# Layer normalisation moved to GpSimd, a wider prologue, a reordered tail and a deeper weight prefetch in a two-layer transformer kernel

## The chip, the cores and the metric

The kernel runs on one core of a Trainium2 chip. The core has five engines that work side by side, each with its own queue: TensorE (PE in the profile; PEld is its weight load) multiplies matrices into PSUM, VectorE (DVE) and ScalarE (ACT) do elementwise work and read PSUM, GpSimd (POOL) does elementwise work in SBUF, and SyncE (SP) issues the DMA transfers, in order. Engines wait for each other through semaphores. The metric is the device time of one execution in microseconds (us), as the median of several runs.

## The reference

The program is two layers, each of an attention block and a feed-forward block, over x of 2048 rows and 512 columns (bf16), with 32 heads of 16 columns and 1792 hidden columns. The layers share their weights:

```python
h = layernorm(x)                       # no scale or shift
q, k, v = split(h @ wqkv)              # 32 heads of 16
x = x + concat(softmax(q @ k.T / 4) @ v) @ wo
x = x + silu(layernorm(x) @ w1) @ w2
```

Most of the elementwise work is the exponential of the scores: 2048 x 2048 for each of 32 heads and two layers, 268 million values.

## The kernel before

**Blocks and steps.** Scores are made transposed, in blocks of 128 keys by 512 queries, four heads at a time: four matmuls of 32 rows side by side on TensorE. A *step* of the main loop handles one key tile for four heads. Three of its four blocks go through ScalarE's exp (one 512-wide, bank `s1`, and one 1024-wide, two banks of `s2`; `exp`, L1182). The fourth, the *d block*, goes through VectorE (`emit_d`, L1091, bank `sd`): it writes the power of two as integer bits into a tile `d_y`, and GpSimd makes two more terms of each pair of d blocks (`other_terms`, L1112, tiles `d_z`); P@V on TensorE (`o_ps`, L960) adds the three terms with scaled copies `VB` of V. A list made in `plan` (L880 on) says which blocks belong to which step. `D_LEAD` = 4: d blocks are made four steps ahead of the others, and those of the first four steps are exps, in step 0. `NO_D` = 12: the blocks of steps 5 to 12 have no d block; all four go through ScalarE there, the second 512-wide one in the bank `sd`, while VectorE starts in that bank on the blocks that come later.

**Background work.** Everything else (projections of K, Q and V, layer norms, output projections, feed-forward) is cut into parts and placed between the steps. `Background` holds the parts in three lists (`outs`, the main queue, `side`), and in each step the loop near its end asks `heads` for candidates and places those that `fits` accepts. `Model` carries the planner's times of each engine for this; its order is written into the queues when the program is built, and the engines then follow it. `bg.ensure` places what a step can't do without.

**Layer norm.** `ln_stats` makes mean and variance on VectorE (L419, L421) and `rstd` on GpSimd with two small instructions (L423, L424). `ln_apply` (L430) normalises one 128x512 tile on VectorE; it works on 513 columns, for which each x tile has one more column, set to zero (L340). The result `xn` has three buffers and goes through a DMA transpose on SP's queue (`transpose`, L329) into `xnT` or `fT`.

**Prologue.** Before the main loop, x of the first 512 rows is loaded in two halves, and the weights in the order K, Q, V; then x of the next chunk. TensorE runs 56 small warm-up matmuls. The four tiles are normalised on VectorE, transposed on TensorE into two PSUM banks of two tiles each (`t_ps`, L1159), copied by ScalarE three times and by VectorE once (L1160), and K and Q of the first head group follow as whole 512-wide projections (`proj_k`, `proj_q`). `proj_q` masks Q twice on VectorE straight from PSUM (L524), for each head group of the first chunk.

**Feed-forward weights.** w1 comes in 14 tiles of 128 columns with three buffers. `next_w1` (L690 on) issues the load of tile ft+2 when the matmuls of tile ft are placed; two tiles are there when a feed-forward begins. In layer 1, from the third unit on, w1 stays in SBUF (`w1_here`).

**Tail.** After the last step `tail` (L785 on) does the last 256 rows alone: transposes of the attention output, the output projection (`out_add`, L638: projection in PSUM, VectorE adds x), statistics of both tiles together, normalise, transposes, then per hidden tile h, tanh on ScalarE (L665), product on VectorE (L668) and the second matmul three tiles behind, and the output. Warm-up matmuls fill gaps of TensorE.

The softmax here doesn't subtract the row's maximum and nothing guards it: scores larger than these inputs give would overflow.

## Time and profile before

| | us |
|---|---|
| median of three runs (1551.96 to 1555.56) | 1552.83 |
| the profiled execution | 1553.61 |
| its span, first to last instruction | 1551.8 |
| ScalarE busy / TensorE / GpSimd / VectorE | 1510.2 / 1456.6 / 1143.1 / 1036.6 |
| first exp starts | 16.07 |
| last P@V starts | 1523.21 |
| ScalarE, 1024-wide exps: 1013 in the normal steps, mean | 1.329 |
| ScalarE, 512-wide exps: 1013, mean | 0.902 |
| VectorE, d_y: 1012, mean | 0.690 |
| GpSimd, d_z 128x1024: 1012, about | 1.045 |
| VectorE, normalise: 64, shortest / median / longest | 0.374 / 0.484 / 1.251 |

Instructions of one engine overlap in the profile, so that the sum of durations is more than the busy time; what one instruction costs its engine is read from the distance between starts. A line of the order of time gives the start, the duration, the engine, the line of the kernel, the operation, the tiles written and read, and in brackets how long the engine was idle before it and what ended that.

### The profile page before, as it was taken

Reading aid. Unit: us, or ns where it says so; the run is one execution under the profiler, and the core shown is the slowest. Engines: PE = TensorE matmul, PEld = TensorE weight load, DVE = VectorE, ACT = ScalarE, POOL = GpSimd, SP = SyncE. Lnnn points to the kernel's source line nnn. Section 1 sums busy time; section 2 is a strip of 40 time slices with the busy share of each in tenths; the row PEclk is TensorE's granted clock in tenths of the full one; section 3 lists DMA queues with packets and bytes.
Section 4 is the critical chain, followed back from the end, with each engine's and each line's share of the span. In section 5 each row is a group of like instructions: output and inputs, shape, how many; then the busy total and the mean of one; then the engine's idle time right before and its main releaser. Section 6 shows DMA issues by size and latency. Waiting matters only on the chain. (4 is left out here: it accounts for less than half of the span.)

```text
span 1551.8 us, 39817 instructions
## 1 busy us (share of the span) xinstructions
PE 1456.6 (94%) x15947; PEld 535.6 (35%) x16056; DVE 1036.6 (67%) x1714; ACT 1510.2 (97%) x2185; POOL 1143.1 (74%) x1245
## 2 busy tenths in 40 slices
PE   8999999899989999899999999998999899999997
PEld 3222332232222332223332233322344344444544
DVE  5877667657676766666676667676567656665663
ACT  6999999999999999999999999999999999999994
POOL 2888777678876888678876678776778677777771
PEclk9999999999999999999999999999999999999999
DMA  4110012102121111211112010121023212000100
GB/s 136 36 28 2 5 36 61 43 15 45 39 49 32 33 24 39 52 28 41 19 40 45 22 35 5 28 49 42 18 47 89 54 25 40 21 21 16 22 14 10
DMA packets 144489, 54.42 MB, mean 35 GB/s; under 512 B 123312, under 2 KB 143792, under 8 KB 144304
## 3 DMA queue, kind: packets, MB, share of 16 engines
q1 hardware_dynamic: 144304, 51.88, 15.0%
q8 instruction: 125, 2.05, 0.6%
q14 instruction: 60, 0.49, 0.1%
HBM read 26.21 MB, written 4.19 MB: 20 GB/s over the span
## 5 line engine op out<-in xcount | busy, mean ns | idle before, releaser
L1182 ACT ACTIVATE p_sb<-s_ps 128x512 bf16<-128x512 f32 x2026 | 1469.2, 1115 | 2.1 <-PE d_ps L924 1.7
L1091 DVE TENSOR_SCALAR d_y<-d_ps 128x512 uint16<-128x512 f32 x1012 | 698.1, 690 | 440.3 <-PE d_ps L924 385.0
L924 PE MATMUL s_ps<-QT,KT 32*128 32x512 bf16 (+1 forms) x3852 | 642.7, 337 | 53.1 <-ACT p_sb L1182 39.1
L924 PEld LDWEIGHTS <-KT 32*128 32x128 bf16 x5120 | 202.2, 91 | 608.8 <-issue 567.5
L924 PE MATMUL d_ps<-QT,KT 32*128 32x512 bf16 (+1 forms) x1268 | 389.9, 339 | 3.4 <-DVE d_y L1091 2.8
L960 PE MATMUL o_ps<-p_sb,VA 128*32 128x512 bf16 (+1 forms) x3807 | 312.1, 343 | 7.1 <-ACT p_sb L1182 1.1
L960 PEld LDWEIGHTS <-VA 128*32 128x32 bf16 x5120 | 120.2, 95 | 136.8 <-issue 104.6
L960 PE MATMUL o_ps<-d_y,VA 128*32 128x512 f16 (+1 forms) x1268 | 154.2, 337 | 0.0
L960 PEld LDWEIGHTS <-VB 128*32 128x32 f16 x2536 | 98.2, 97 | 41.9 <-issue 0.5
L749 PE MATMUL f_ps<-w_sb,hT 128*128 128x512 bf16 x370 | 102.6, 382 | 5.5 <-issue 4.8
L665 ACT ACTIVATE t_sb<-h_ps 128x512 f32<-128x512 f32 x105 | 93.4, 889 | 3.6 <-PE h_ps L486 3.1
L668 DVE SCALAR_TENSOR_TENSOR hT<-t_sb,h_ps 128x512 bf16<-128x512 f32 x105 | 72.0, 685 | 22.2 <-ACT t_sb L665 20.6
L960 PE MATMUL o_ps<-w_qkv,zero 128*32 128x512 bf16 (+1 forms) x1356 | 73.3, 335 | 0.0
L1071 DVE CAST oT<-o_ps 128x512 bf16<-128x512 f32 (+1 forms) x80 | 46.0, 574 | 7.7 <-PE o_ps L960 7.7
L749 PEld LDWEIGHTS <-hT 128*128 128x128 bf16 x420 | 31.3, 97 | 47.9 <-issue 25.4
L419 DVE BATCH_NORM_STATS2 st<-x 128x6 f32<-128x512 bf16 x64 | 43.6, 681 | 1.9 <-DMA x<-in_A_x_dram 1.9
L430 DVE TENSOR_SCALAR xn<-x,mv,rstd 128x513 bf16<-128x513 bf16 x64 | 42.0, 670 | 1.9 <-POOL rstd L424 1.7
L960 PEld LDWEIGHTS <-zero 128*32 128x32 bf16 x1356 | 28.1, 95 | 27.1 <-issue 20.0
L486 PE MATMUL k_ps<-xnT,w_qkv 128*128 128x512 bf16 x128 | 36.0, 393 | 1.3 <-DMA xnT<-xn 0.7
L486 PE MATMUL q_ps<-xnT,w_qkv 128*128 128x512 bf16 x136 | 36.7, 388 | 0.0
L627 POOL TENSOR_TENSOR attn<-ot,rec 128x128 bf16<-128x128 bf16 (+1 forms) x61 | 31.2, 511 | 6.0 <-DVE rec L620 6.0
L486 PE MATMUL v_ps<-w_qkv,xnT 128*128 128x512 bf16 x112 | 33.0, 382 | 1.6 <-issue 0.6
(2279 smaller groups left out, 2074.9 us busy)
## 6 DMA issues: line engine op xcount, KB each, us to landing
QT<-q SPq DMA_DIRECT2D x240, 16.0 KB, 1.8
x<-in_A_x_dram SPq DMA_DIRECT2D x7, 512.0 KB, 4.3
wo<-in_A_wo_dram SPq DMA_DIRECT2D x6, 512.0 KB, 3.8
out_dram<-x SPq DMA_DIRECT2D x16, 128.0 KB, 1.7
w_sb<-in_B_w_dram SPq DMA_DIRECT2D x1, 1792.0 KB, 13.2
w_qkv<-in_A_wqkv_dram SPq DMA_DIRECT2D x3, 512.0 KB, 6.8
w_here<-in_B_w_dram SPq DMA_DIRECT2D x3, 512.0 KB, 5.1
ot<-oT SPq DMA_TRANSPOSE x61, 2.4
```

What stands on the lines that cost most here:

```text
L419: nc.vector.bn_stats(st[:], x_sb[c][:, i, :])
L430: nc.vector.tensor_scalar(out=wide[:].rearrange("p (a b) -> p a b", b=19), in0=x_wide[c][:, D * i : D * (i + 1) + 1], scalar1=mv[:, 0:1], ...
L486: nc.tensor.matmul(ps.rearrange("p (t q) -> p t q", q=P) if len(r.shape) == 3 else ps, lhsT=lhs(ct), rhs=r, start=(ct == 0), stop=(ct == C ...
L627: scale(out=attn[L, qc][:, 0:n, P * g : P * (g + 1)].rearrange("p t (j s) -> p t j s", s=32)[:, :, :, 16 * par : 16 * par + 16], in0=att[: ...
L665: nc.scalar.activation(t_sb, h_ps, ACT.Tanh, scale=0.5)
L668: nc.vector.scalar_tensor_tensor(out=out, in0=t_sb, scalar=1.0, in1=h_ps, op0=ALU.add, op1=ALU.mult)
L749: nc.tensor.matmul(y_ps, lhsT=hT[:, ft, k * P : (k + 1) * P], rhs=w2_sb[:, ft, :], start=(ft == 0), stop=(ft == FT - 1),)
L924: nc.tensor.matmul(out[:, P * len(q) * n : P * len(q) * (n + 1)], lhsT=KT[L, kts // 4][r, g, (kts % 4) * P : (kts % 4 + 1) * P], rhs=QT[g] ...
L960: nc.tensor.matmul(o_tiles[key][32 * j : 32 * j + 32, 0:w], lhsT=lhsT[k] if real else zero[:], rhs=rhs[:, w * k : w * (k + 1)], start=(n[j ...
L1071: nc.vector.tensor_copy(out=o, in_=o_tiles[key][:, 0 : o.shape[-1]])
L1091: nc.vector.tensor_scalar(out=pr["y"][:, len(pr["ds"]), :], in0=s_ps[:], scalar1=float(1024 * SCALE * math.log2(math.e)), scalar2=float(10 ...
L1182: nc.scalar.activation(p_sb, s_ps, ACT.Exp, bias=-SHIFT * math.log(2.0) + math.log(EXP_SUM), scale=float(SCALE),)
```

## The change

The normalise of the main loop runs on GpSimd (`ln_apply` takes an engine); the prologue and the tail keep VectorE. It works on 512 columns, the extra column of x is gone, and `xn` has four buffers. Of the second to fourth head group's Q, VectorE makes one copy and GpSimd the two masked ones (`q_masked`). The blocks of steps 5 to 8 keep four exps; for steps 9 to 12 the four d blocks become two 1024-wide exps placed ahead of step 9 (`lead`, `p_lead`), so the bank `sd` is VectorE's from step 9 on. In the prologue each of the four transposed tiles has its own bank, K and Q are made in halves of two tiles each, eight warm-ups stand between, and x of the second chunk is loaded ahead of V's weights. In the main loop the `side` list goes ahead of the main queue until the second chunk is normalised. w1's tiles are loaded three ahead, each load placed after the product of its unit. In the tail x is added in PSUM by a fifth matmul with the identity, statistics are read from PSUM tile by tile, each with its own `rstd`, and ScalarE copies the sum into x.

```diff
-    def heads(self, now):
-        return [
-            self.outs[0] if self.outs else None,
-            self.head(now),
-            self.prime(self.side[0]) if self.side else None,
-        ]
+    def heads(self, now, side_first=False):
+        heads = [self.head(now), self.prime(self.side[0]) if self.side else None]
+        return [self.outs[0] if self.outs else None, *heads[:: -1 if side_first else 1]]
...
-    xnpool = ctx.enter_context(tc.tile_pool(name="xnpool", bufs=3))
+    xnpool = ctx.enter_context(tc.tile_pool(name="xnpool", bufs=4))
...
-    def transpose(out, in_):
+    def transpose(out, in_, made=0.0):
         nc.sync.dma_start_transpose(out=out, in_=in_)
         if bg.model:
+            bg.model.sp = max(bg.model.sp, made)
             bg.model.transpose()
...
-        x_wide[c] = xpool.tile([P, 4 * D + 1], BF16, name="x", tag="x")
-        nc.gpsimd.memset(x_wide[c][:, 4 * D :], 0.0)
-        x_sb[c] = x_wide[c][:, 0 : 4 * D].rearrange("p (t d) -> p t d", t=4)
...
         nc.sync.dma_start(w_qkv[:, :, D * i : D * (i + 1)], wq[:, :, D * i : D * (i + 1)])
-    load_x(1)
+        if i == 0:
+            load_x(1)
...
+    def ln_apply(c, i, mv, rstd, engine=nc.vector):
+        xn = xnpool.tile([P, D], BF16, name="xn", tag="xn")[:]
+        engine.tensor_scalar(
+            out=xn,
+            in0=x_sb[c][:, i, :],
             scalar1=mv[:, 0:1],
             scalar2=rstd,
             op0=ALU.subtract,
...
     def ln_chunk(c, dst, tiles=range(4)):
         for i in tiles[::2]:
             mv, rstd = stats.pop((c, i))
-            yield part(need=("rstd", c, i))
             for u in range(2):
-                yield part(0.45, need=("xn", xn_count[0] - XN_BUFS))
-                xn = ln_apply(c, i + u, mv[:, u, :], rstd[:, u, :])
-                transpose(dst[:, i + u, :, :], xn)
+                yield part(need=("xn", xn_count[0] - XN_BUFS))
+                xn = ln_apply(c, i + u, mv[:, u, :], rstd[:, u, :], nc.gpsimd)
+                transpose(dst[:, i + u, :, :], xn, bg.model and bg.model.pool_busy(0.62))
                 bg.done["xn", xn_count[0]] = bg.model.landed
                 xn_count[0] += 1
...
+        nc.vector.tensor_copy(out=KT[L, c][:, g, :], in_=k_ps)
+    def q_masked(g, q_ps):
+        QT[g] = qpool.tile([P, 2, 512], BF16, name="QT", tag=f"QT{g}")
+        engine = nc.vector
+        if g > 0:
+            q = qpool.tile([P, 512], BF16, name="q", tag="q", bufs=2)[:]
+            nc.vector.tensor_copy(out=q, in_=q_ps)
+            q_ps, engine = q, nc.gpsimd
+            if bg.model:
+                bg.model.pool_busy(1.25)
+        for par in range(2):
+            engine.tensor_scalar_mul(out=QT[g][:, par, :], in0=q_ps, scalar1=masks[par][:, 0:1])
...
         if (L, c) == (0, 0):
-            QT[g] = qpool.tile([P, 2, 512], BF16, name="QT", tag=f"QT{g}")
-            for par in range(2):
-                nc.vector.tensor_scalar_mul(
-                    out=QT[g][:, par, :], in0=q_ps, scalar1=masks[par][:, 0:1]
-                )
-                if par == 0 and g > 0:
-                    yield part(0.65, held=True)
+            q_masked(g, q_ps)
             return
...
-        if (L, u) < (1, 1) or ft + 2 < FT:
-            load_w1((ft + 2) % FT)
-        elif ft + 2 == FT:
-            for k in (FT - 2, FT - 1):
-                w1_here[k] = w1pool.tile([P, CT, P], BF16, name="w1", tag="w1")[:]
-                load(w1_here[k], B_w1.rearrange("(ct p) f -> p ct f", p=P)[:, :, k * P : (k + 1) * P])
-        return w1.pop(ft)
+        if (L, u) < (1, 1) or ft + 3 < FT:
+            load_w1((ft + 3) % FT)
+    def take_w1(L, u, ft):
+        w = w1.pop(ft)
+        if (L, u) == (1, 1) and ft >= FT - 2:
+            w1_here[ft] = w
+        return w
...
-            load_w1(0)
-            load_w1(1)
+            for ft in range(3):
+                load_w1(ft)
         yield part(need=("fT", L, u))
...
-                h_ps = yield from h_whole(next_w1(L, u, ft), fT)
+                h_ps = yield from h_whole(take_w1(L, u, ft), fT)
...
+            if n == 1:
+                next_w1(L, u, ft)
...
+        z_ps = [bank("z_ps") for _ in range(2)]
+        ln = []
         for n, i in enumerate(tiles):
-            run(out_add(c, i, aT[:, n, :, :]))
-        warm(8)
-        mv, rstd = run(ln_stats(c, tiles))
+            for ct in range(CT):
+                nc.tensor.matmul(
+                    z_ps[n], lhsT=aT[:, n, ct, :], rhs=wo[0][:, ct, :], start=(ct == 0), stop=False
+                )
+            nc.tensor.matmul(z_ps[n], lhsT=ident[:], rhs=x_sb[c][:, i, :], start=False, stop=True)
+            ln.append(run(ln_stats([z_ps[n]])))
+            nc.scalar.copy(out=x_sb[c][:, i, :], in_=z_ps[n])
+        warm(7)
         for n, i in enumerate(tiles):
-            xn = ln_apply(c, i, mv[:, n, :], rstd[:, n, :])
+            mv, rstd = ln[n]
+            xn = ln_apply(c, i, mv[:, 0, :], rstd[:, 0, :])
             turn_tile(xn, fT[:, n, :, :], COPY[1 - n])
-            if n == 0:
-                warm(2)
+            warm(2)
...
@@ -880,31 +897,37 @@
         blocks = [[(*r[0:5], kt, j) for j in range(4)] for r in runs for kt in r[5]]
         d_of = [b[b[0][5] % 4] for b in blocks]
         steps = [(d_of[0:D_LEAD], [])]
-        for i in range(D_LEAD, NO_D):
-            d_of[i] = None
+        lead = d_of[NO_D - D_LEAD : NO_D]
         pv = {}
         for i, b in enumerate(blocks):
-            a = [b[(b[0][5] + k) % 4] for k in range(1, 4 + (d_of[i] is None))]
-            steps.append((a, [d for d in d_of[i + D_LEAD : i + D_LEAD + 1] if d]))
+            whole = D_LEAD <= i < NO_D - D_LEAD
+            a = [b[(b[0][5] + k) % 4] for k in range(1, 4 + whole)]
+            steps.append((a, d_of[i + D_LEAD : i + D_LEAD + 1] if i + D_LEAD >= NO_D else []))
             pv.setdefault(max(i // 2 * 2 + 4, i // 2 + 7 if i < 8 else 0), []).extend(
-                [(i + 1, k) for k in range(len(a))] + [(0, i)] * (i < D_LEAD)
+                [(i + 1, k) for k in range(len(a))]
+                + [(0, i)] * (i < D_LEAD)
+                + [("lead", i + D_LEAD - NO_D)] * (NO_D - D_LEAD <= i < NO_D)
             )
-        return steps, pv
...
-        for i in range(56):
+        for i in range(50):
             nc.tensor.matmul(w_ps[:, 0:P], lhsT=ident[:], rhs=ident[:], start=True, stop=True)
         new_v(0, 0)
         xnT[0, 0] = xslot(0, "xnT")
-        ln = [run(ln_stats(0, (i, i + 1))) for i in (0, 2)]
-        for i, tag in ((0, "s1"), (2, "sd")):
+        ln = [run(ln_stats([x_sb[0][:, i + u, :] for u in range(2)])) for i in (0, 2)]
+        t_ps = psum["s"].tile([P, 2, 1024], BF16, name="t_ps", tag="s2", bufs=2)
+        t_ps = [t_ps[:, 0, :], t_ps[:, 1, :]] + [
+            psum["s"].tile([P, 1024], BF16, name="t_ps", tag=tag, bufs=1)[:] for tag in ("s1", "sd")
+        ]
+        for i in range(4):
             mv, rstd = ln[i // 2]
-            t_ps = psum["s"].tile([P, 1024], BF16, name="t_ps", tag=tag, bufs=1)[:].rearrange(
-                "p (u c q) -> p u c q", c=CT, u=2
-            )
-            for u, copy in enumerate((nc.scalar.copy, nc.vector.tensor_copy if i else nc.scalar.copy)):
-                xn = ln_apply(0, i + u, mv[:, u, :], rstd[:, u, :])
+            xn = ln_apply(0, i, mv[:, i % 2, :], rstd[:, i % 2, :])
+            for ct in range(CT):
+                nc.tensor.transpose(
+                    t_ps[i][:, ct * P : (ct + 1) * P], xn[:, ct * P : (ct + 1) * P], ident[:, :]
+                )
+            copy = nc.vector.tensor_copy if i == 3 else nc.scalar.copy
+            copy(out=xnT[0, 0][:, i, :, :].rearrange("p c q -> p (c q)"), in_=t_ps[i][:, 0:512])
+            if i == 1:
+                for _ in range(8):
+                    nc.tensor.matmul(w_ps[:, 0:P], lhsT=ident[:], rhs=ident[:], start=True, stop=True)
+        KT[0, 0] = kslot(0, [P, NG, 512], BF16, "KT")
+        kq_ps = [bank("k_ps"), bank("q_ps")]
+        for i in (0, 2):
+            for k in range(2):
                 for ct in range(CT):
-                    nc.tensor.transpose(t_ps[:, u, ct, :], xn[:, ct * P : (ct + 1) * P], ident[:, :])
-                copy(out=xnT[0, 0][:, i + u, :, :], in_=t_ps[:, u, :, :])
-        bg.done["ln", 0, 0] = 0.0
-        bg.add(("k", 0, 0, 0), proj_k(0, 0, 0))
-        bg.add(("q", 0, 0, 0, 0), proj_q(0, 0, 0))
-        bg.ensure(("q", 0, 0, 0, 0))
+                    nc.tensor.matmul(
+                        kq_ps[k][:, P * i : P * (i + 2)].rearrange("p (t q) -> p t q", q=P),
+                        lhsT=w_qkv[:, ct, D * (1 - k) : D * (1 - k) + P],
+                        rhs=xnT[0, 0][:, i : i + 2, ct, :],
+                        start=(ct == 0),
+                        stop=(ct == CT - 1),
+                    )
+        nc.scalar.copy(out=KT[0, 0][:, 0, :], in_=kq_ps[0])
+        q_masked(0, kq_ps[1])
+        bg.done.update({("ln", 0, 0): 0.0, ("k", 0, 0, 0): 0.0, ("q", 0, 0, 0, 0): 0.0})
...
+            if t == NO_D - D_LEAD + 1:
+                p_lead = xslot(3, "p_lead")[:].rearrange("p t c q -> p t (c q)")
+                for i in (0, 2):
+                    s2 = score_pair()[:]
+                    for k in range(2):
+                        score([lead[i + k]], [s2[:, k, :]])
+                    exp(flat(p_lead[:, i : i + 2, :]), flat(s2))
+                    m.pair()
+                p_tiles["lead"] = [p_lead[:, i, :] for i in range(4)]
...
-                for item in bg.heads(t):
+                for item in bg.heads(t, ("ln", 0, 1) not in bg.done):
...
-        warm(4, s_ps[:, 1, :])
+        warm(2, s_ps[:, 1, :])
```

## The prediction

> **What bounds the kernel now.** I read the page's first part, then the waits of ScalarE, then the order of time around each wait.
>
> ```profile
> span 1551.8 us, 39817 instructions
> PE 1456.6 (94%) x15947; PEld 535.6 (35%) x16056; DVE 1036.6 (67%) x1714; ACT 1510.2 (97%) x2185; POOL 1143.1 (74%) x1245
> ```
>
> ScalarE is busy 97% of the span, and nearly all of it is the exps. From the starts in the trace a 512-wide exp holds it 0.494 us, a 1024-wide one 0.912, so a normal step takes 1.406. No part of the change makes an exp cheaper. What can be won is the 16.1 us before the first exp, the 28.6 after the last, and the stalls between: the ScalarE starts are further apart than 0.494 or 0.912 by 14.0 us in all between 16 and 1522 us.
>
> ```profile
> ACT t_sb L665 <- PE h_ps L486: 3.1, 3, 1.5
> ACT p_z L1182 <- PE s_ps L924: 1.2, 5, 0.3
> ACT p_sb L1182 <- PE d_ps L924: 1.7, 1, 1.7
> ```
>
> These lines (total, times, longest) name the three kinds of stall. The order of time shows what lies behind each.
>
> The start:
>
> ```profile
> 8.18 0.59 ACT L1160 COPY xnT<-t_ps 128x512 bf16<-128x512 bf16 x1 [5.94 <-PE t_ps L1159]
> 10.37 0.38 PE L1159 MATMUL t_ps<-ident,xn 128*128 128x128 bf16 x4 [0.94 <-ACT xnT L1160]
> 10.85 0.42 DVE L1160 COPY xnT<-t_ps 128x512 bf16<-128x512 bf16 x1 [2.04 <-PE t_ps L1159]
> 11.33 1.86 PE L486 MATMUL k_ps<-xnT,w_qkv 128*128 128x512 bf16 x4 [0.58 <-DVE xnT L1160]
> 14.84 0.75 DVE L524 TENSOR_SCALAR QT<-q_ps,mask_130 128x512 bf16<-128x512 f32 x1 [3.56 <-PE q_ps L486]
> 16.07 1.94 ACT L1182 ACTIVATE p_pre<-s_ps 128x1024 bf16<-128x1024 f32 x2 [2.26 <-PE s_ps L924]
> ```
>
> Transposes wait for a bank that ScalarE still copies, and K and Q run at 0.43 us a matmul, twice their time elsewhere (the granted clock is 0.5 from 11.2 to 14.6).
>
> A VectorE normalise caught behind GpSimd:
>
> ```profile
> 82.52 2.37 DVE L430 TENSOR_SCALAR xn<-x,mv,rstd 128x513 bf16<-128x513 bf16 x2
> 82.57 1.04 POOL L1112 TENSOR_SCALAR d_z_1264<-d_y 128x1024 uint16<-128x1024 uint16 x1
> 83.70 1.04 POOL L1112 TENSOR_SCALAR d_z_1266<-d_y 128x1024 uint16<-128x1024 uint16 x1
> 85.53 0.37 PE L924 MATMUL d_ps<-QT,KT 32*128 32x512 bf16 x1 [1.04 <-DVE d_y L1091]
> 88.14 2.11 ACT L1182 ACTIVATE p_sb<-s_ps 128x512 bf16<-128x512 f32 x3 [1.75 <-PE d_ps L924]
> ```
>
> Alone a normalise takes 0.41; these two end with the GpSimd instruction beside them. The next d_y is late, then its bank, then the scores, then the exp.
>
> A weight load behind others in SP's queue:
>
> ```profile
> 634.98 0.58 SPq L334 DMA_DIRECT2D w_10623<-in_B_w_dram  x1
> 637.63 1.04 PE L486 MATMUL h_ps<-fT,w_10623 128*128 128x512 bf16 x4 [2.35 <-DMA w_10623<-in_B_w_dram]
> 638.71 0.60 ACT L665 ACTIVATE t_sb<-h_ps 128x512 f32<-128x512 f32 x1 [1.54 <-PE h_ps L486]
> ```
>
> And the end:
>
> ```profile
> 1528.73 0.69 DVE L638 TENSOR_TENSOR x<-x,y_ps 128x512 bf16<-128x512 bf16 x1 [0.17 <-PE y_ps L486]
> 1531.42 0.71 POOL L424 TENSOR_TENSOR rstd<-rstd,half 128x2 f32<-128x2 f32 x1
> 1534.26 3.20 PE L841 MATMUL h_ps<-fT,w_here 128*128 128x256 bf16 x16 [0.52 <-DVE fT L812]
> ```
>
> **The change part by part.** The sum is made against the profiled run, 1553.6 us (span 1551.8); the median of the runs is 1552.8, 0.8 lower.
>
> A, prologue. With four banks each transpose waits only for its normalise. Second tile: normalised at 7.48, transposed by 7.9, copied by 8.85 behind the first copy. Third and fourth: rstd at 8.04, normalised by 8.8, copied by 9.5 (0.42 on VectorE). K and Q of the first two tiles, 8 half-wide matmuls, run from 8.9; at full clock (0.216 per 512, so 0.108) until 9.8, the second half until 10.65. The first mask ends at 11.45 (0.75), the scores give the first exp at 11.9. Against 16.07: -4.1. At the half clock of this row the 16 matmuls take 3.5 and the exp comes at 13.65: -2.4. I take -4.1, since they now stand before the 11.2 at which the clock fell; a little earlier statistics or copies could make it -4.5. V's weights move behind x(1) in SP's queue: 2.5 MB have landed by 10.1 us, so these (2.6 MB in) come about 10.5; V is wanted near 14. Cost 0; without that cover it would be 1.5 (0.5 MB at 350 GB/s).
>
> B, early blocks. The eight steps with four ScalarE blocks run from 23.82 to 41.04, 17.2 us. In their place: four at 2 x 0.494 + 0.912 = 1.90, four at 1.406, two wide exps at 0.912: 15.05. So -2.2, of which only 0.15 is ScalarE's work; the rest is the wait for the bank that VectorE's d_y shared with an exp, in the last five. Ends: 0, if DVE's d_y at the new steps is as late, and -2.4.
>
> C, normalise off VectorE. Stalls that follow a normalise longer than 0.6 us: 0.35 (62.5), 0.18 (79.5), 2.02 (85.2), 0.11 (88.6), 0.40 (255.8), 0.45 (1302.4), 0.40 (1374.2). Sum -3.9, all gone when the instruction is. Ends: -1.25 (the late three) and -3.9.
>
> D, normalise on GpSimd: what is late next. No row shows it. Its form lies between VB (128x136, 0.31) and d_z (128x1024, 1.05); a line through both gives 0.62 at 512, and 0.08 between instructions 0.70. A pair of d_z takes 2.24 in 2.81 (two steps), so GpSimd recovers only 0.57 per pair. The order of the changed kernel puts, between its third and tenth pair of d_z, 16 d_z (17.9), eight normalises (5.6), three rstd (3.1), two of the Q masks that also moved here (1.4) and V's memsets (1.1): 29.1 us, while seven pairs arrive in 14 x 1.406 = 19.7. The tenth pair is 9.4 late. Its P@V comes six steps (8.4) after it is made (seven before the change, as the first VectorE block moves one step), and in the trace of before such a count leaves 1.85 less than it says: 6.6 us of cover, 2.8 short; 0.5 more behind V's scaling soon after. These 3.3 fall on TensorE in about four P@V groups, where it has some 0.3 us a step to spare: I take +2.0, at 55 to 75 us. Ends by the two rows: at 0.39 each 0.2, so 0; at 1.13 the ten extra instructions cost 4.3 more in that window (7.6), and eight of the later groups of four, with 0.5 to 1.1 us to spare, lose about 0.8 each: +14. The normalise is nearest the middle of the two sizes, so 0.62.
>
> The Trainium skill (GPSIMD Engine Reference, section 4.1) speaks against the move: elementwise work on a tile belongs to VectorE. Its section 3.1 has 512 elements at 769 ns in a tight loop; by that, 0.15 more for each of ten instructions, D would be an estimated +3.5 and the sum -13.3. No row of before shows which holds.
>
> What hangs on the move besides: the DMA transposes of each normalised tile stand in SP's queue behind GpSimd now, and QT copies, ot transposes and weight loads behind them. SP waits for a normalise already (60.9 us, 15 times). K, V and h are placed only once the planner sees the tile landed, so the cover is the next chunk's distance; the weights get theirs from E. The Q masks 1 to 3 leave VectorE a 0.69 copy instead of 2 x 0.75; the first is needed eight steps later.
>
> E, weights. Stalls of the tanh for a w1 tile: 1.17 (448), 2.00 (636), 1.27 (1045, with a 3.4 us clock dip). Three tiles are now there when an FFN starts, and each later load has three units of 3.3 us for a landing of 2.2 to 2.6. -4.4; the other end is 0, if SP stands that long behind a GpSimd normalise.
>
> F, tail. Two warm-ups fewer bring the transposes from 1525.83 to 1525.55 (attn ends 1525.48). z takes 5 matmuls a tile: 1526.5 to 1528.7. Statistics straight from z (0.69 + 0.18) end at 1529.6, the second rstd (1.0) at 1530.7, as the first ran beside it; normalise, transposes and copy (0.35, 0.4, 0.45) put h at 1532.05 against 1534.26: -2.2. ScalarE's copy of z into x lies beside rstd. Ends: -1.0 (if the rstds or copies queue) and -3.0 (0.55 more if h then finds the full clock, and no delay at z).
>
> Sum: -4.1 - 2.2 - 3.9 + 2.0 - 4.4 - 2.2 = -14.8. 1553.6 - 14.8 = 1538.8, 0.8 less for a median: 1538.
>
> **The rivals.**
> 1. GpSimd becomes the bound (the other side). With every normalise at 1.3 us instead of 0.62, the early window costs about 10 and the later groups of four 18 more: +28, in all +11.5, 1564. It decides from D = 16.8, which is about 1.1 us per normalise, just above d_z's own 1.05. For it: 84% of GpSimd busy at 50 to 75 us (20.9 of 25). Against: half the elements of a d_z. 5%.
> 2. The middle of that: at 1.0 to 1.05 us D is 8 to 14, the time 1544 to 1550. 10%.
> 3. Only the ends gain. A and F hold (-6.3) while the planner's new order makes as many stalls as B, C and E remove: 1546.5. For it: every step of the stream is placed anew. Against: the causes of those stalls are named above and gone. 12%.
> 4. The start falls into the half clock (A = -2.4), the rest as forecast: 1540. 8%, and beside it my sum: 65%.
>
> **How the numbers follow.** Main and case 4 (73%) give 1534 to 1543 of their own. Rivals 2 and 3 reach 1550; of these and 1 I leave out the far part, so 1531 to 1548 for 8 in 10; the low end is all terms at their good ends with D at 0 (-18.2, 1534.6) and 3.5 for small stalls of the old order. A measurement of this kernel tells 0.2% (3 us) from no change. Faster: 0.73 + 0.12 + half and more of rival 2 = 0.91; same 0.04; slower 0.05.
>
> **What would show it.** A: first exp near 12 us, K and Q at 0.11 per half. B: ScalarE from the ninth step on at 1.41. C: no gap after 255, 1302, 1374. D: the normalise's mean on GpSimd near 0.62, and P@V waits on d_z between 55 and 80 us. E: no tanh waiting for w1. F: h of the tail 8.8 us after the last P@V starts, not 11.05. Wrong if a normalise on GpSimd is above 1 us, or if d_z waits stand at every chunk.

## The result and the profile after

The changed kernel is slower: 1597.2 us (median, 1595.9 to 1599.6) against 1552.4 us for the kernel before, a ratio of 1.0287 with a 95% interval of 1.0268 to 1.0306. The forecast was 1538 us. Its profiled execution took 1595.9 us, with this at the head of the page:

```profile
span 1594.1 us, 39873 instructions
PE 1479.4 (93%) x16004; PEld 534.1 (34%) x16004; DVE 999.9 (63%) x1651; ACT 1513.8 (95%) x2185; POOL 1270.2 (80%) x1299
```

ScalarE is busy about as long as before (1513.8 us for 1510.2), in a span that is 42.3 us longer. GpSimd has 127 us more to do and VectorE 37 us less. The waits of ScalarE (total, times, longest) say what it stood for:

```profile
ACT p_sb L1222 <- PE d_ps L947: 47.5, 29, 8.5
...
ACT p_sb L1222 <- PE s_ps L947: 2.6, 1, 2.6
```

The first line was 1.7 us before, in one wait; now there are 29. TensorE, which the exps wait for, has these two lines in its own waits:

```profile
PE o_ps L983 <- POOL d_z L1135: 30.4, 18, 5.1
PE d_ps L947 <- POOL QT L521: 8.2, 1, 8.2
```

Both end on GpSimd. Its groups of instructions (busy time, mean ns) hold the reason:

```profile
L431 POOL TENSOR_SCALAR xn<-x,mv,rstd 128x512 bf16<-128x512 bf16 x58 | 119.7, 2074 | 0.3
...
L521 POOL TENSOR_SCALAR QT<-q,mask 128x512 bf16<-128x512 bf16 x6 | 9.3, 1564 | 7.2 <-DVE q L516 7.2
```

A normalise takes 2.07 us on GpSimd, where the forecast had 0.62: twice the time of a d_z (1.04), which is twice as wide. The four of a chunk are issued in a row. Two places in the order of time show what such a row does. First the early one:

```profile
44.82 8.25 POOL L431 TENSOR_SCALAR xn<-x,mv,rstd 128x512 bf16<-128x512 bf16 x4
...
53.15 2.17 POOL L1135 TENSOR_SCALAR d_z<-d_y 128x1024 uint16<-128x1024 uint16 x2
55.31 3.11 POOL L521 TENSOR_SCALAR QT<-q,mask 128x512 bf16<-128x512 bf16 x2
56.93 0.58 PE L947 MATMUL d_ps<-QT,KT 32*128 32x512 bf16 x1 [8.20 <-POOL QT L521]
...
59.09 1.51 ACT L1222 ACTIVATE p_sb<-s_ps 128x512 bf16<-128x512 f32 x2 [8.46 <-PE d_ps L947]
```

The masked Q of a head group stands behind four normalises and a pair of d_z. The scores wait for it, and the exps for the scores. Later the same row of four delays the d_z, at each of the ten rows of four after 125 us:

```profile
260.66 8.25 POOL L431 TENSOR_SCALAR xn<-x,mv,rstd 128x512 bf16<-128x512 bf16 x4
...
268.99 6.66 POOL L1135 TENSOR_SCALAR d_z<-d_y 128x1024 uint16<-128x1024 uint16 x6
270.09 0.40 PE L983 MATMUL o_ps<-d_z,VB 128*32 128x512 f16 x4 [2.37 <-POOL d_z L1135]
...
271.22 0.43 PE L983 MATMUL o_ps<-d_z,VB 128*32 128x512 f16 x2 [0.73 <-POOL d_z L1135]
...
272.26 1.51 ACT L1222 ACTIVATE p_sb<-s_ps 128x512 bf16<-128x512 f32 x2 [3.19 <-PE d_ps L947]
```

P@V waits 2.37 and 0.73 us for d_z made behind the row, the next scores are queued behind P@V, and ScalarE stands for 3.19 us. Counted from the starts on ScalarE as in the forecast, the stalls between the first exp and the last are now 62.9 us against 14.0: 23.2 against 5.3 between 24 and 125 us, 39.3 against 8.3 after that. With the two ends (3.5 us won at the start, 3.3 at the end) this gives +42.1, the 42.3 us of the span. The granted clock is 0.79 in the mean of 30 to 100 us (0.98 before); in experiment 2, with the same order of every queue but short GpSimd instructions, it is 0.93. So most of its fall comes with these stalls; what it adds to them no run parts.

### The profile page after: what moved, and what is told of

Read it like the earlier page. It is cut to its first block, busy times and chain, and to the rows that moved or that the text cites. A ratio compares the mean times of both kernels' runs of the same rounds, so it can differ in the third digit from the quotient of the medians.

```text
span 1594.1 us, 39873 instructions
## 1 busy us (share of the span) xinstructions
PE 1479.4 (93%) x16004; PEld 534.1 (34%) x16004; DVE 999.9 (63%) x1651; ACT 1513.8 (95%) x2185; POOL 1270.2 (80%) x1299
## 3 DMA queue, kind: packets, MB, share of 16 engines
q1 hardware_dynamic: 143248, 51.62, 13.5%
## 5 line engine op out<-in xcount | busy, mean ns | idle before, releaser
L1135 POOL TENSOR_SCALAR d_z<-d_y 128x1024 uint16<-128x1024 uint16 x1012 | 1056.0, 1043 | 274.4 <-DVE d_y L1114 114.8
L947 PE MATMUL d_ps<-QT,KT 32*128 32x512 bf16 (+1 forms) x1268 | 395.6, 344 | 8.8 <-POOL QT L521 8.2
L983 PE MATMUL o_ps<-p_sb,VA 128*32 128x512 bf16 (+1 forms) x3819 | 317.2, 346 | 6.5 <-ACT p_sb L1222 1.1
L983 PE MATMUL o_ps<-d_z,VB 128*32 128x512 f16 (+1 forms) x2536 | 255.0, 341 | 31.9 <-POOL d_z L1135 30.4
L431 POOL TENSOR_SCALAR xn<-x,mv,rstd 128x512 bf16<-128x512 bf16 x58 | 119.7, 2074 | 0.3
L759 PE MATMUL f_ps<-w_sb,hT 128*128 128x512 bf16 x420 | 111.5, 382 | 0.0
L672 ACT ACTIVATE t_sb<-h_ps 128x512 f32<-128x512 f32 x105 | 89.4, 852 | 3.4 <-PE h_ps L719 2.0
L487 PE MATMUL h_ps<-fT,w 128*128 128x512 bf16 x336 | 89.2, 389 | 1.7 <-DMA fT<-xn 1.4
L487 PEld LDWEIGHTS <-w 128*128 128x128 bf16 x336 | 26.4, 99 | 42.2 <-issue 20.6
```

The source lines that it names most:

```text
L431: engine.tensor_scalar(out=xn, in0=x_sb[c][:, i, :], scalar1=mv[:, 0:1], scalar2=rstd, op0=ALU.subtract, op1=ALU.mult,)
L487: nc.tensor.matmul(ps.rearrange("p (t q) -> p t q", q=P) if len(r.shape) == 3 else ps, lhsT=lhs(ct), rhs=r, start=(ct == 0), stop=(ct == C ...
L672: nc.scalar.activation(t_sb, h_ps, ACT.Tanh, scale=0.5)
L759: nc.tensor.matmul(y_ps, lhsT=hT[:, ft, k * P : (k + 1) * P], rhs=w2_sb[:, ft, :], start=(ft == 0), stop=(ft == FT - 1),)
L947: nc.tensor.matmul(out[:, P * len(q) * n : P * len(q) * (n + 1)], lhsT=KT[L, kts // 4][r, g, (kts % 4) * P : (kts % 4 + 1) * P], rhs=QT[g] ...
L983: nc.tensor.matmul(o_tiles[key][32 * j : 32 * j + 32, 0:w], lhsT=lhsT[k] if real else zero[:], rhs=rhs[:, w * k : w * (k + 1)], start=(n[j ...
```

## The experiments

The runs came in five batches, each with its own runs of the kernel before (medians 1552.7, 1553.7, 1554.6, 1553.1 and 1553.1 us), so ratios are given beside the times. "Base" says which kernel was edited.

**1. What a normalise costs on GpSimd, and why.** Base: before. Nine instructions on GpSimd in the tail, at 256, 512 and 1024 columns:

```diff
+    nc.gpsimd.tensor_scalar(out=..., in0=x2[:, 0:n], scalar1=m_, scalar2=r_, op0=ALU.subtract, op1=ALU.mult)
+    nc.gpsimd.tensor_scalar_mul(out=..., in0=x2[:, 0:n], scalar1=masks[0][:, 0:1])
+    nc.gpsimd.tensor_scalar(out=..., in0=x2[:, 0:n], scalar1=1.5, scalar2=0.0, op0=ALU.mult, op1=ALU.add)
```

> The kernel before, with nine more GpSimd instructions in the tail whose results nothing uses: tensor_scalar on 256, 512 and 1024 bf16 columns, each once with two per-partition scalars read from SBUF (subtract, mult: the normalise's own form), once with one such scalar (mult, the Q mask's form) and once with plain numbers (mult, add). If the per-partition scalars are what makes the normalise take 2.07 us: at 512 about 2.07, 1.56 and 0.62; at 1024 about 4.0, 3.0 and 1.05; at 256 about 1.1, 0.8 and 0.4. If it is the bf16 type or the place in the stream: the three forms agree with each other at each width. The whole time says nothing here (the tail is longer by these instructions).

Measured: 1552.9 us, one run. Part of GpSimd's order of time at the end:

```profile
1536.17 2.08 POOL L832 TENSOR_SCALAR probe<-x,mv,rstd 128x512 bf16<-128x512 bf16 x1
1538.35 1.57 POOL L837 TENSOR_SCALAR probe<-x,mask 128x512 bf16<-128x512 bf16 x1
1540.01 0.62 POOL L840 TENSOR_SCALAR probe<-x 128x512 bf16<-128x512 bf16 x1
```

The tile, its type and its size are the same in the three lines. With two scalars read per partition (mean, rstd) the instruction takes 2.08 us, with one (the mask) 1.57, with plain numbers 0.62. At 256 columns the three are 1.36, 0.93 and 0.40, at 1024 3.79, 2.85 and 1.04. The forms differ in their operations too (subtract and multiply; multiply; multiply and add), but the one with plain numbers has as many as the normalise and is the cheapest, so it is not their count. The forecast's 0.62 is exactly right for the form of the two rows it was drawn from, and that form is not the normalise's.

**2. Is this price the loss?** Base: after. Normalise and masks 1 to 3 keep their place and size on GpSimd, but multiply by a plain number; normalising and masking are left out by it.

```diff
-                xn = ln_apply(c, i + u, mv[:, u, :], rstd[:, u, :], nc.gpsimd)
+                xn = ln_fixed(c, i + u)   # nc.gpsimd.tensor_scalar(..., scalar1=2.0, scalar2=0.0, ...)
...
-            engine.tensor_scalar_mul(out=QT[g][:, par, :], in0=q_ps, scalar1=masks[par][:, 0:1])
+            engine.tensor_scalar(out=QT[g][:, par, :], in0=q_ps, scalar1=0.5, scalar2=0.0, ...)
```

> The changed kernel, but the GpSimd normalise of the main loop multiplies x by a plain number instead of subtracting the mean and multiplying by rstd, and the six Q masks on GpSimd multiply by a number: the same instruction count, order and sizes, without per-partition scalars (the normalisation and masking proper are left out). If the loss is the length of these GpSimd instructions alone: each takes about 0.62 us, and the time is that of my sum, 1540 (1534 to 1546). If the new order or another part loses the time: over 1575. If GpSimd is slow at bf16 512 wide in any form: the instructions stay near 2 us and the time near 1597.

Measured: 1545.3 us, ratio 0.9959 (0.9944 to 0.9974). The order of every queue is that of after; only the form of 64 instructions differs, and with it their duration: 0.62 us each. A row of four takes 2.36 us in place of 8.25, and TensorE no longer waits for d_z or for the masked Q. The order of time and the waits have these lines; the second is all that is left of TensorE's waits for GpSimd in the main loop:

```profile
42.54 2.36 POOL L443 TENSOR_SCALAR xn<-x 128x512 bf16<-128x512 bf16 x4
...
PE o_ps L995 <- POOL VB L596: 2.2, 2, 1.8
```

52 us go with the price (51 by the ratios). Stalls after 125 us are 0.4 us in all. But 8.0 us of stalls stay between 24 and 125, 4.0 of them just before 74.8 us, so that the time, inside the expected range, is 5 us above its middle.

**3. The normalise back on VectorE.** Base: after.

```diff
-                yield part(need=("xn", xn_count[0] - XN_BUFS))
-                xn = ln_apply(c, i + u, mv[:, u, :], rstd[:, u, :], nc.gpsimd)
-                transpose(dst[:, i + u, :, :], xn, bg.model and bg.model.pool_busy(0.62))
+                yield part(0.45, need=("xn", xn_count[0] - XN_BUFS))
+                xn = ln_apply(c, i + u, mv[:, u, :], rstd[:, u, :])
+                transpose(dst[:, i + u, :, :], xn)
```

> The changed kernel with the normalise of the main loop back on VectorE (plain 512 columns, planned at 0.45 us as before, waiting for rstd); the Q masks stay on GpSimd. If the move of the normalise is the loss: 1543 (1538 to 1549), that is the kernel before less A, B, E and F, with the normalise's stalls (3.9 us in the kernel before) still there. If the loss is shared with the Q masks: 1550 to 1565. If another part is the loss: over 1575.

Measured: 1550.5 us, ratio 0.9985 (0.9974 to 0.9996). So 47 us of the loss are the normalise, but what is left (with the masks still on GpSimd) is worth 2 us, where A, B, E and F were forecast at 12.9 together. Stalls are 13.7 us between 24 and 125 and 3.9 after: something early is still wrong.

**4. The move alone.** Base: before, with only the normalise moved (the reverse of the diff of experiment 3).

> The kernel before with only the normalise of the main loop on GpSimd (three xn buffers, plain 512 columns). If the length of that instruction is the loss: 56 x 1.45 us more than planned on GpSimd, stalls at each group of four, 1600 (1590 to 1612). If the loss needs the other parts (the new order, the masks, fewer steps between making and using a block): under 1565.

Measured: 1618.4 us, ratio 1.0428 (1.0406 to 1.0449), above the expected range. Beside P@V's waits for d_z (15.7 us) the feed-forward now waits 20.0 us for its transposed tiles (eight times, up to 3.6), which SP can issue only when GpSimd has made them. In after these waits are 2.5 us in all; no run shows which of the other parts hides them there.

**5. Normalise and masks on VectorE.** Base: experiment 3, and the Q masks as in before.

```diff
         for par in range(2):
-            engine.tensor_scalar_mul(out=QT[g][:, par, :], in0=q_ps, scalar1=masks[par][:, 0:1])
+            nc.vector.tensor_scalar_mul(out=QT[g][:, par, :], in0=q_ps, scalar1=masks[par][:, 0:1])
```

> The kernel after with both the normalise of the main loop (plain 512 columns) and the six Q masks back on VectorE; prologue, early blocks, tail and weights stay as in after. In the run with only the normalise moved back (1550.5 us) the stream of exps on ScalarE still lost 18.0 us between its steps, 14.1 of them between 24 and 92 us (before: 5.4 there). Theory M, the masks on GpSimd (two of 1.56 us, one after the other, for each of three head groups) are what is left of the loss: most of these 8.7 us come back, 1541 to 1545 us. Theory P, the order of the early work is at fault (four VectorE blocks less leave VectorE and GpSimd to start later, so that the eight VB copies at 72 to 78 us, 2.96 us together, stand behind d_z operations and a P@V waits for them while K's projection and the next scores are queued behind it on TensorE): the stall of 5 us at 72 to 78 us stays and only the small ones go, 1546 to 1550 us.

Measured: 1548.2 us, ratio 0.9956 (0.9939 to 0.9974): in the range of theory P. Between 24 and 125 us 9.7 us of stalls are left, and 7.5 of them have one place:

```profile
68.12 4.41 POOL L1130 TENSOR_SCALAR d_z<-d_y 128x1024 uint16<-128x1024 uint16 x4
...
72.54 2.98 POOL L579 TENSOR_SCALAR VB<-VA 128x136 f16<-128x136 bf16 x8
72.90 1.36 PE L978 MATMUL o_ps<-d_z,VB 128*32 128x512 f16 x2 [2.70 <-POOL VB L579]
...
74.20 1.89 PE L487 MATMUL k_ps<-xnT,w_qkv 128*128 128x512 bf16 x4
...
76.71 1.51 ACT L1217 ACTIVATE p_sb<-s_ps 128x512 bf16<-128x512 f32 x2 [5.30 <-PE s_ps L942]
```

The scaled copies VB of the second chunk's V stand behind four d_z. A P@V waits for them, K's projection is queued behind it and takes 1.89 us (1.04 in experiment 8, without this wait), then come the scores, and ScalarE has waited 5.30 us.

**6. Without the early blocks.** Base: experiment 5, with the hunks of `plan`, `lead`, `p_lead`, `pair` and `side_first` undone.

> The run before (normalise and masks on VectorE) with the part of the four early blocks undone too: the last four VectorE blocks of the opening keep their VectorE form and no extra ScalarE exps are put in. What is left of the change is the prologue (first exp 3.5 us earlier), the tail (about 3.3 us shorter) and the weights three ahead (4.4 us of waits gone). Theory M: the early blocks were worth the 2.2 us of the forecast, so this is about 2 us slower than the run before it: 1543 to 1548 us. Theory P: the early blocks bring the stall with them, so this is faster than the run before it, by 3 us or more: 1540 to 1544 us. Were all three terms that are left to pay in full, 1552.5 less 3.5, 3.3 and 4.4 us = 1541.3 us.

Measured: 1545.9 us, ratio 0.9941 (0.9923 to 0.9959). This is theory P's sign: the early blocks cost 2.3 us, where 2.2 were to be gained. But it is less than the 3 us that theory P asked for, and the time itself lies in theory M's range. The intervals of the two ratios overlap, since both hold the spread of the kernel before; the six runs of each, taken in one batch, hardly do (1543.8 to 1547.4 against 1547.0 to 1549.0). The stalls between 24 and 125 us fall from 9.7 to 5.4. This run is the prologue, the tail and the weights (with the 512 columns and the fourth `xn` buffer): by the ratio 9.2 us won, where the forecast had 10.7 for the three.

**7. The early blocks alone, and the weights alone.** Base: before, with those hunks only, or with the hunks of `next_w1`, `take_w1` and the three first loads only.

> The kernel before with only the four early VectorE blocks made as wide ScalarE exps (and the order of side work that goes with it). The forecast: 2.2 us less, 1550 to 1551 us. Theory P (the early blocks bring a stall of several us, since VB's copies and the d_z before them come late for the P@V that reads them): 1554 to 1559 us.

Measured: 1558.9 us, ratio 1.0035 (1.0019 to 1.0052). Slower, as theory P has it: the stall at VB is there without any other part of the change (6.3, 1.4 and 0.5 us, ending at 81.8, 84.6 and 86.6 us). TensorE's one long wait for GpSimd is again the one for VB:

```profile
77.67 2.96 POOL L580 TENSOR_SCALAR VB<-VA 128x136 f16<-128x136 bf16 x8
...
PE o_ps L969 <- POOL VB L580: 3.2, 1, 3.2
```

> The kernel before with only the weights of the first MLP product taken three ahead in place of two. Waits on these loads in the kernel before: four of 0.8 to 2.0 us on ScalarE. If they are on the path as the forecast has it: 4.4 us less, 1548 to 1549 us. If another thing is late next, or the halved clock after such a wait costs nothing: 1551 to 1553 us.

Measured: 1550.0 us, ratio 0.9974 (0.9961 to 0.9987), 4.0 us less by the ratio (2.0 to 6.1), where 4.4 were forecast. The time itself lies between the two expected ranges; the kernel before was 1 us slower in this batch than they assume.

**8. VB made tile by tile.** Base: experiment 5. A VB copy needs one tile of V, so the eight need not wait for the fourth.

```diff
             bg.done["v", L, c, tq] = 0.0
-        scale_v(L, c)
+            scale_v(L, c, tq)      # the two copies of this tile
```

> The kernel after with normalise and Q masks on VectorE, early blocks kept, and one more edit: the eight GpSimd copies that make VB of a chunk are issued two at a time, after each of the four V tiles, in place of all eight after the last tile. In the run without this edit (1548.25 us) the P@V at 69.8 us waits 3.2 us for the first of them, which stands behind four d_z operations, and ScalarE then loses 5.6, 1.4 and 0.5 us between 70 and 82 us. Theory P (the early blocks of the change bring this stall, by the place of the VB copies in GpSimd's queue): it goes, and 5 to 7.5 us with it, 1541 to 1543.5 us. Rival: the d_z operations are late themselves and the P@V waits for them just as long: 1547 to 1549 us.

Measured: 1544.7 us, ratio 0.9939 (0.9923 to 0.9955), 2.6 us below experiment 5 by the ratio. The stalls between 24 and 125 us fall from 9.7 to 4.1, by as much as theory P said (5.6); 1.2 us of other stalls came in later, with the order planned anew, and the time lies 1.2 us above theory P's range, still below the rival's. No P@V waits for VB any more. So the place of VB is shown as the cause of most of that stall; 2.3 us stay at the same place, where K's projection now stands behind a P@V that waits 0.5 us for V itself.

> The same edit on the run without the early blocks (1545.9 us), which had no stall at VB. If the early blocks are worth the forecast's 2.2 us once their stall is gone, this is 2 us slower than the run above it: 1543.5 to 1546 us. If they are worth nothing, the two agree within 1 us.

Measured: 1546.2 us, ratio 0.9946 (0.9929 to 0.9963). With the stall gone the run with the early blocks is 1.5 us faster, 1.1 by the ratio: between what the two theories asked for. The two intervals overlap nearly whole, so that no gain is shown clear of noise, and a small one is not excluded.

**9. Would a planner that knows the price have kept the gain?** Base: after.

```diff
-                transpose(dst[:, i + u, :, :], xn, bg.model and bg.model.pool_busy(0.62))
+                transpose(dst[:, i + u, :, :], xn, bg.model and bg.model.pool_busy(2.1))
...
-                bg.model.pool_busy(1.25)
+                bg.model.pool_busy(3.15)
```

> The kernel after with one edit in the planner's model alone: a normalise on GpSimd is booked at 2.1 us in place of 0.62, and the two Q masks at 3.15 us in place of 1.25, so that P@V, transposes and projections are planned behind the queue as it really is. If the loss comes from an order that was planned on too small a price (P@V and scores put where their d_z or QT is not there yet), most of the 40 us between after and the run with the normalise on VectorE come back: 1555 to 1575 us. If it comes from GpSimd's time itself (74% busy before, and 2.07 us for each of 58 normalises in lumps of four), the order can't help: 1590 to 1605 us.

Measured: 1604.7 us, ratio 1.0332 (1.0312 to 1.0352). The four still stand in a row (8.26 us at 262): their part has no VectorE time, so the planner finds that it fits and issues all four at once. P@V still waits for d_z nearly as long:

```profile
PE o_ps L983 <- POOL d_z L1135: 24.7, 18, 3.2
```

So a loss through the planner's too small price is not what the run shows, but it doesn't settle whether the row of four or the sum is the cost. In the next run the planner lets 2.5 us of VectorE's time pass between two normalises (base: `true_costs`).

```diff
+                yield part(need=("gap", xn_count[0]))
...
+                bg.done["gap", xn_count[0]] = bg.model.dve + 2.5
```

> The run with the true prices in the planner's model (1604.7 us), where the four normalises of a chunk still stood one behind the other in GpSimd's queue (8.26 us), with one more edit: a normalise may be issued only 2.5 us of the planner's VectorE time after the last, so that a pair of d_z stands between most of them. Worked out from the same 0.56 us: the d_z behind the first normalise is 2.1 us late, behind the fourth 6.4 us, in place of 8.3 us. Theory queue: some of the loss comes back, 1580 to 1597 us. If the lump plays no part: 1600 to 1608 us.

Measured: 1603.6 us, ratio 1.0325 (1.0307 to 1.0343): by its time, no help. But the stalls have changed their place, as TensorE's waits show:

```profile
PE k_ps L490 <- DMA xnT<-xn: 22.3, 2, 13.5
PE o_ps L986 <- POOL d_z L1138: 10.3, 14, 1.7
```

P@V's waits for d_z fall from 24.7 to 10.3 us, the longest from 3.2 to 1.7. What came in their place is two waits of a K projection for transposes of normalised tiles, up to 13.5 us long. At the shorter one SP's queue shows three transposes between 772.7 and 782.6, which wait for the four normalises (issued between 770.6 and 785.6), then eight transfers of QT, then the fourth transpose. At the longer one, which ends at 977.5, three of the four normalises still stand in a row (6.19 us from 968.86), and the projection waits for the last tile. So parting the row takes more than half of the d_z waits away, but the time stays: with 58 normalises of 2.07 us on GpSimd the tiles come late instead. A run with few normalises that stand in rows of four would part row and sum; there is none.

**10. Fewer normalises on GpSimd.** Base: experiment 8, with every fourth, or every second, normalise of the main loop on GpSimd.

```diff
+                pool = xn_count[0] % 4 == 3          # two_in_four: % 2 == 1
+                yield part(0.0 if pool else 0.45, need=("xn", xn_count[0] - XN_BUFS))
+                xn = ln_apply(c, i + u, mv[:, u, :], rstd[:, u, :], nc.gpsimd if pool else nc.vector)
```

> The fastest version so far (normalise and masks on VectorE, VB by tile, 1544.7 us) with every fourth normalise of the main loop on GpSimd, at 2.07 us each, some 14 in place of 58. Between two pairs of d_z (2.25 us with their gaps) GpSimd has some 0.56 us free in each 2.81 us of two exp steps. Theory queue (a lump has to be longer than the wait that the P@V of these d_z blocks can bear): one normalise alone puts a d_z back by 2.15 us at most and four by 8.3 us, so one is worth little: 1544 to 1550 us. Theory sum (each normalise costs its share of the 47 us that all 58 cost on this base): a quarter, 1555 to 1558 us.

Measured: 1541.1 us, ratio 0.9921 (0.9906 to 0.9937), the fastest of all versions, 12 us below the kernel before. In GpSimd's order of time one normalise has this effect:

```profile
243.83 2.08 POOL L431 TENSOR_SCALAR xn<-x,mv,rstd 128x512 bf16<-128x512 bf16 x1
245.99 11.15 POOL L1131 TENSOR_SCALAR d_z<-d_y 128x1024 uint16<-128x1024 uint16 x10
257.92 2.17 POOL L1131 TENSOR_SCALAR d_z<-d_y 128x1024 uint16<-128x1024 uint16 x2 [0.78 <-DVE d_y L1110]
```

The five pairs of d_z behind it run without a gap, the sixth waits for its input again: the delay is made up in 12 us. No P@V waits for a d_z in the whole run. The theory that each normalise costs its share of the 47 us (1555 to 1558 us) falls. By the ratio the time is 2.8 us below experiment 8, which the two intervals don't separate.

> The run with one normalise of four on GpSimd (1541.1 us), with every second one there in place of every fourth: some 28 of 2.07 us each, two in each chunk, apart from each other by one on VectorE. In the steady stretch of that run GpSimd's pairs of d_z start every 3.30 us and leave 1.13 us free. Theory queue: two put d_z back by 4.2 us at most, one was borne without a stall, four were not (waits of P@V on d_z of up to 5.1 us); if the wait that can be borne lies between 2.1 and 4.2 us, stalls of 1 to 2 us at each chunk, 1545 to 1560 us; if over 4.2 us, 1539 to 1543 us. Theory sum: half of what 58 cost, 1564 to 1570 us.

Measured: 1557.0 us, ratio 1.0018 (1.0004 to 1.0032). Between the two ends, but not for the expected reason:

```profile
PE d_ps L943 <- DMA QT<-q: 4.1, 1, 4.1
PE o_ps L979 <- POOL VB L580: 2.5, 1, 2.5
```

There is again no wait of P@V for a d_z: two normalises a chunk are borne too, as far as the d_z go. ScalarE loses 8.0 us between 971 and 981, where Q of a head group is projected too late (its copy ends at 971.3, and its 24 transfers take SP until 981.4), and 4.9 at 71 to 80, where VB is late once more. Why the parts came out in this order is open, and so is whether the 16 us above the run with one of four have to do with GpSimd's time at all.

## Why the prediction was wrong

**D, the price of a normalise on GpSimd, is the step that failed.** It was put at 0.62 us, with +2.0 us for the whole move; it measured 2.07, and the move cost 46.9 us for the normalise and some 4.5 for the masks. The line through VB (0.31) and d_z (1.05) gave 0.62 by size. Both rows read plain numbers (`scalar1=w`, `scalar1=float(off)`); the normalise reads two scalars per partition, and experiment 1 puts that at 3.3 times. The upper end of 1.13 was too low as well. A nearer row stood in the profile before: GpSimd's product of attention output and reciprocals (`attn<-ot,rec`, a tensor as its second operand) takes 0.40 at 128x128 and 0.62 at 128x256; a line through these two gives 1.06 at 512, and the second doubled 1.24, on either side of the 1.1 at which the forecast's own rival 1 decides. That would not have been enough either, but it would have put the change near no gain. (The sum of rival 1, 28 less 16.8, is +11.2, not 11.5.)

The counting behind D had the right direction, and its early sum comes out close. With 2.07 in place of 0.62 for eight normalises, and 1.56 for the two masks, the 29.1 us of work become 42.6 (8 x 1.45 and 2 x 0.94 more); less the 19.7 in which seven pairs arrive and the cover of 6.6 us, this gives 16.3 of early loss. Of the 23.2 us of stalls between 24 and 125 us, 8.0 stay when the price is gone (experiment 2), so that 15.2 belong to it. That they agree so well is partly luck: the sum counts a late pair of d_z alone, and the largest of these stalls (8.46 us at 59.1) is one for which it had no term. It is the scores' wait for the masked Q behind the row of four; the forecast called the masks safe, as needed eight steps later. The next (6.08 us at 84.3) does come from a P@V that waits for d_z, 5.07 us. The later groups of four, with their 0.5 to 1.1 us to spare, would by the same counting lose about 5 us each (4 x 1.45 less that); the ten rows of four after 125 us lose 1.8 to 4.4 us each, 3.6 in the mean. Rival 1 had this mechanism and its sign, with 5%, at a price of 1.3.

The Trainium skill was weighed in D. Its rule (GPSIMD Engine Reference, section 4.1: elementwise work on VectorE) agrees with 2.07 us here against a mean of 0.69 on VectorE in experiment 3. The same row calls operations with one input roughly line-rate on GpSimd; the normalise, with one tile and two scalars per partition as its inputs, is not that here. Its 769 ns for 512 elements (section 3.1), there the best case of a tight loop, fits none of the three forms at 512 columns: 0.62, 1.57 and 2.08.

**B** had the wrong sign. The exps no longer wait for the bank `sd`, but other waits come in the steps after (0.7, 1.6, 0.3 and 1.1 us between 30 and 45 us in `blocks_alone`, 3.6 in all, where the same stretch of the kernel before had 2.4), and the new order puts VB, the next GpSimd work with a deadline, behind d_z (8.2 us). Alone it costs 5.4 us by the ratio (2.9 to 8.1), where 2.2 less were forecast. The step's ends of 0 and -2.4 left out a loss, though nothing in the profile excluded one; V's scaling was priced at 0.5 us, inside D. Rival 3 named this mechanism in general (a new order makes as many stalls as it removes).

**A** was right in sign and inside its range: the first exp comes at 12.60 for 11.9, 3.5 us earlier than in the profile before. Part of that size is luck: the clock had fallen in that one execution of the kernel before, and where it had not (last section) the same count gives about 1.5.

```profile
8.31 0.38 PE L1182 MATMUL t_ps<-ident,xn 128*128 128x128 bf16 x4 [0.67 <-ACT xnT L1186]
...
9.42 0.60 PE L1195 MATMUL k_ps<-xnT,w_qkv 128*128 128x256 bf16 x4
...
12.60 1.94 ACT L1222 ACTIVATE p_pre<-s_ps 128x1024 bf16<-128x1024 f32 x2 [1.08 <-PE s_ps L947]
```

K and Q ran at the full clock (1.00 granted from 9 to 12.5 us), at 0.11 a half as forecast. The transpose of the second tile still waited 0.67 us for ScalarE's copy of the first, where the step had each transpose wait for its normalise alone. The program holds that wait; the first two of the four tiles are halves of one allocation (`t_ps[:, 0, :]` and `t_ps[:, 1, :]`), which would explain it, but no run parted them. **F** was under-sized: h of the tail starts 9.2 us after the last P@V (forecast 8.8, before 11.05), but from there the 16 matmuls take 1.92 us in place of 3.20, at the full clock, and the whole end is 3.3 us shorter. **E** was right: 4.0 us for 4.4 (experiment 7), and TensorE, which waited 2.3 and 1.5 us for loads of w1 before, has no wait on one in after. So was **C** in what it removes: with the price gone (experiment 2) the late stalls, at 255, 1302 and 1374 us, are below 0.1; the early ones can't be told from the other stalls there.

A, E and F together were forecast at -10.7 and measured at -9.2 (experiment 6; -6.4 to -12.0 by its interval). Put back in one after the other, by the ratios, the early blocks add 2.3, the masks on GpSimd 4.5 and the normalise there 46.9, each uncertain by some 3 us. That these lead to the +44.6 of the result is no test, since each is the difference of two neighbours in one chain.

## What to carry to other kernels

Price an instruction that moves to another engine by a row with the same kinds of operands, not only the same size; where no such row exists, measure the instruction by itself, or let the bound reach far beyond the nearest row. An engine that is 75% busy on average can bear a short instruction (2 us here, made up in 12) and still not four in a row: look at the longest run of work that goes in ahead of its deadlines, beside the sum. Which of the two decided here is not parted: 14 and 29 normalises cost no wait for d_z, but 58 cost as much with their rows parted as in rows. And a step that starts VectorE's or GpSimd's stream elsewhere also moves everything queued behind it, so follow the next work with a deadline on that queue, here V's scaled copies.

## What the hardware showed that was not expected

- GpSimd's cost by columns depends on where its scalars come from: between 256 and 1024 columns it is 3.2 ns a column with two scalars per partition ((3.79 - 1.36) / 768), 2.5 with one, 0.83 with plain numbers.
- The old prologue's first exp is not at one time. Five profiles of kernels that share it have it at 16.07, 15.62 and 15.75 us with a granted clock of 0.50 to 0.60 between 11.2 and 14.6 us, and at 14.05 and 14.27 with a clock of 1.00. The new prologue's lies between 12.51 and 13.06 in the eleven profiles that have it, with a clock of 1.00 from 6 to 16 us in each. So A is worth between 1.0 and 3.6 us by the run, and single executions of the old prologue can differ by 2 us before the first exp. The Trainium skill (TensorE: Matmul & The Clock Gate, Part 1) says that the gate judges TensorE's activity in windows of about 3.4 us that run free of the kernel's start; the dip here is 3.4 us long and comes or not by the execution, which agrees.
